# Attention with a spatial-gating MLP on one core: a stored order of the pieces, and weight bits in PSUM

## The chip, the cores and the metric

The kernel runs on one core of one Trainium2 chip. The metric is the device time of one execution in microseconds, and lower is better. A core has a TensorE (PE in the profile, with its weight loads as PEld), a VectorE (DVE), a ScalarE (ACT), a GpSimd (POOL) and a SyncE (SP), each with its own queue of instructions that it works off in order; SP here only issues DMAs. Engines wait for one another through semaphores.

## The reference

Eight batches, each with 8 heads of 64 over 576 positions. Attention is the sum of two parts, and an MLP with a gate over positions follows:

```python
q_d = q.reshape(B, H, Sd, 4, D).mean(axis=3)          # k_d and v_d alike; Sd = 144
out_up = np.repeat(sm_attn(q_d, k_d, v_d), 4, axis=2)  # softmax attention on the means of 4
scores = np.where(abs(i - j) < 4, scale * q @ k.T, -1e9)
out_local = softmax(scores) @ v                        # a band of 7 keys
x = out_up + out_local                                 # heads side by side: 576 x 512
h = gelu(x @ w_in)                                     # tanh form, 512 x 1024
u, v = h[..., :512], h[..., 512:]
v_n = (v - mean(v)) / sqrt(var(v) + 1e-6) * g_ln
v_s = einsum('ts,bsd->btd', w_sg, v_n) + b_sg[None, :, None]
out = x + (u * v_s) @ w_out
```

`w_in` and `w_out` arrive as 64-bit floats, so the kernel turns their two 32-bit words into one 32-bit float itself.

## The kernel before

**Pieces.** The work is cut into about 2200 pieces, each a few instructions on one engine. A piece has a name, the engines that can run it, the pieces it comes after, the buffers it takes and those it gives back. For a pair of heads `g` (32 of them, four for each batch), the pieces are: `lq lk lv lw` loads of q, k and two forms of v; `qs ks vs` sums of four; `S` scores of the band and `Y` scores of the means (PE); `ma mb` mask; `mx my` maxima; `nx ny` the scaled negative maxima used as bias; `ea eb ec` exponentials on ACT with their sums; `rc` reciprocal of the sums; `np nq` norms; `T U t` transposes on PE; `pa pb pc pe` their evacuation from PSUM; `d` and `D` products with v on PE; `od` mean part evacuated; `xa xb` the two parts added into x; `xh xl xc` x split into a high float and a low rest, since each large product is made of three (high times high, low times high, high times low). The first six pairs are "early": they take the mask and the sum of v into PE products.

For a batch `b`, five `v` products (the first half of the MLP's hidden layer), each followed by gelu `vg`, statistics `vb`, a root on POOL `vp`, `vn`, and a high and a low part `vh vl`; eight `u` products with gelu `ua`; eight gate products `s` with bias `sa` and gate `sm`, then parts `gh gl`; eight output products `o`, added to x (`oa`) and stored (`os`).

**Weights.** `w_in` and `w_out` come in 24 pieces of 128 x 256 (`y0` to `y7`, `z0` to `z7`, `r0` to `r7`). Each runs through `w` (load), `wb` (two DVE instructions, lines 345 and 347: shift and mask the high word into the bit pattern of a float), `wu` (ACT: the low word), `wq` (ACT: a square, for the test of small values), `wf` (DVE, line 361: flush small values to zero), `wt` (POOL or DVE, line 366: add both words), `wh` (high part) and `wl` (low part, line 372). All 24 run in the first batch, beside its attention. The bit pattern is held in a second buffer of the pool R, taken at the load together with the first. The five pieces `q0` to `q4` of the gate's matrix need only a high and a low part.

**Buffers.** Eight PSUM banks (`ps`), ten buffers `X` and forty buffers `R` are handed to the pieces as they come free.

**The order.** A planner, `plan`, runs when the kernel is built. It has a cost in us for each piece on each engine, due times worked back from the period of 70 us for a batch, limits on how many buffers each kind may hold (`CAPS`), and a string `ORDER` of 442 corrections in us to the pieces' latest start times, some with an engine named. It steps through time and gives each engine the ready piece with the earliest latest start. What comes out is a sequence of pieces with engines and buffers; each engine's queue holds its pieces in that sequence.

The lines that matter to the change are 330 to 381 (`weight64`), 541 to 544 (`recip`) and 645 to 686, where the pieces of a pair are declared. Line 788 is the helper of the products u, s and o, line 710 that of v, line 271 the helper of all copies.

Of the kernel before, what the change touches and what calls it, by code (L numbers as in the profile page):

```python
# [50 lines left out]
class Task:  # L51
# [4 lines left out]
    def __init__(self, name, engines, emit, after, takes=(), gives=(), due=None, func=None, mb=0.0, hold=0.0):  # L56
        self.name, self.engines, self.emit, self.due, self.func, self.mb = name, engines, emit, due, func, mb
        self.after, self.takes, self.gives, self.hold = list(after), list(takes), list(gives), hold
        self.kind = name.rstrip("0123456789.")
        if self.kind[0] == "w" and len(self.kind) > 2:  # L60
            self.kind = self.kind[:2]


LAT = 0.16
COLD = 0.8
AHEAD = 25.0
TABLE = 1.3
DMA_LAT, DMA_RATE = 1.9, 0.26

SHARED = dict(np=0.6, nq=0.6, xl=0.6, wb=1.0, wf=1.0, wt=1.0, wl=0.7, wh=1.0, vn=0.3, vh=1.0, vl=0.6,  # L70
              xh=1.0, sm=0.6, gh=1.0, gl=0.6, nx=0.3, ny=0.3)
LONE = ("vp", "xc")


def plan(tasks, sizes, caps, later={}, pinned={}):

    n = len(tasks)
    index = {t.name: i for i, t in enumerate(tasks)}
    succ, left = [[] for _ in tasks], [0] * n
    for i, t in enumerate(tasks):
        for a in set(t.after):
            succ[index[a]].append(i)
            left[i] += 1
    cost = [min(t.engines.values()) + (DMA_LAT + t.mb / DMA_RATE if t.mb else 0.0) for t in tasks]
    order, seen = [i for i in range(n) if not left[i]], list(left)
    for i in order:  # L90
        for j in succ[i]:
            seen[j] -= 1
            if not seen[j]:
                order.append(j)
    assert len(order) == n, [t.name for i, t in enumerate(tasks) if seen[i]][:20]
    due = [1e9 if t.due is None else t.due for t in tasks]
    for i in reversed(order):
        for j in succ[i]:
            due[i] = min(due[i], due[j] - cost[j] - LAT)
    latest = [due[i] - cost[i] + later.get(t.name, 0.0) for i, t in enumerate(tasks)]  # L100
    free = {p: list(range(c)) for p, c in sizes.items()}
    held = {k: 0 for k in caps}
    readers = {}
    for t in tasks:
        for g in t.gives:
            readers[g] = readers.get(g, 0) + 1
    engine_at = {e: 0.0 for t in tasks for e in t.engines}
    func_on, where, given, out = {}, {}, [], []
    dma_at = now = beside = 0.0
    idle = 1.0  # L110
    ready = [max(t.hold, latest[i] - AHEAD) if t.mb else t.hold for i, t in enumerate(tasks)]
    pending = [i for i in range(n) if not left[i]]

    def fits(t):
        need = {}
        for k in t.takes:
            need[k[0]] = need.get(k[0], 0) + 1
            need[k[:2]] = need.get(k[:2], 0) + 1
        return all(len(free[k]) >= c if k in free else k not in caps or held[k] + c <= caps[k]
                   for k, c in need.items())  # L120

    def engines(i):
        e = pinned.get(tasks[i].name)
        return {e: tasks[i].engines[e]} if e else tasks[i].engines


    def queue(e, i):
        total = 0.0
        for j in pending:
            if j != i and ready[j] <= now + 1e-9 and latest[j] < latest[i] and e == home[j]:  # L130
                total += tasks[j].engines[e]
        return total

    home = [min(engines(i), key=engines(i).get) for i in range(n)]
    while len(out) < n:
        while given and given[0][0] <= now + 1e-9:
            k = given.pop(0)[1]
            free[k[0]].append(where[k])
            if k[:2] in caps:
                held[k[:2]] -= 1  # L140
        best = None
        for i in pending:
            t = tasks[i]
            if ready[i] > now + 1e-9 or not fits(t):
                continue
            can = engines(i)
            ends = {e: max(now, engine_at[e]) + c + queue(e, i) for e, c in can.items()} if len(can) > 1 else can
            e = min(ends, key=ends.get)
            if engine_at[e] > now + 1e-9:
                continue  # L150
            key = latest[i] + (TABLE if t.func and func_on.get(e, t.func) != t.func else 0.0)
            if best is None or key < best[0]:
                best = key, i, e
        if best is None:
            times = [x for x in engine_at.values()] + [ready[i] for i in pending] + [g[0] for g in given]
            times = [x for x in times if x > now + 1e-9]
            assert times, ("stuck", sorted(tasks[i].name for i in pending)[:40], free)
            now = min(times)
            continue
        _, i, e = best  # L160
        t = tasks[i]
        pending.remove(i)
        end = now + t.engines[e]
        if e == "V" and t.kind in SHARED:
            end += SHARED[t.kind] * max(0.0, min(end, beside) - now)
        if e == "P" and t.kind not in LONE:
            beside = end
        if e == "T":
            idle = 0.85 * idle + 0.15 * min(1.0, (now - engine_at[e]) / 2.0)
            end += COLD * min(1.0, 3.0 * idle) * t.engines[e]  # L170
        if t.func:
            if func_on.get(e, t.func) != t.func:
                end += TABLE
            func_on[e] = t.func
# [26 lines left out]
wtz0,-42.5, wz1,4.5, wbz2,-37.5, wtz2,90,P wlz2,-57.5,P wz3,10.5, wtz3,17.5, wlz3,87.5,P wz4,8.5, wbz4,-121,
wfz4,14, wtz4,15.5, wz5,13, wuz5,-23.5, wqz5,-33, wtz5,-6,P wz6,-5.5, wfz6,-177, wz7,4, wfz7,-84.5, wr0,38,
wur0,77.5, wfr0,199.5, wtr0,37.5, wr1,-26, wbr1,43.5, wqr1,57.5, wbr2,24, wqr2,-36, wlr2,23,V wr3,-13.5, wbr3,1,
whr3,61.5, wr4,29, wqr4,52.5, wlr4,94.5,V wr5,-24, wbr5,25, wqr5,64, whr5,32.5,A wr6,42, wur6,-38.5, wqr6,-19,
wlr6,78,P wlr7,-18,P whq0,10.5, wlq0,-15,V wq1,10, whq1,-30.5,V wq2,-6, wq3,-11, lq0,-198.5,S lw0,-79,S
# [812 lines left out]
```

## Time and profile before

| | us |
|---|---|
| three runs | 627.39, 627.63, 629.62 |
| their median | 627.63 |
| the profiled execution | 627.54 |
| its span, first to last instruction | 625.8 |

| engine | busy us | share of the span | instructions |
|---|---|---|---|
| PE | 595.5 | 95% | 6600 |
| PEld | 532.9 | 85% | 6600 |
| DVE | 474.2 | 76% | 996 |
| ACT | 364.2 | 58% | 1262 |
| POOL | 275.0 | 44% | 359 |

The mean granted clock of TensorE is 0.988 of full speed. PE's matmuls are pipelined and overlap, and their ends are modelled, so a PE that is busy isn't PE at its peak. A share of busy time is a mean over stages: what a change is worth is read from the stage in which it acts. In a line of the groups stand the kernel's line, the engine, the operation, output and inputs by the program's names with their shapes, the count, then the busy time in us, the mean of one in ns, and the idle time of the engine just before them with what ended it.

### The profile page before, as it was taken

What the parts mean: (1) busy time and instruction counts of PE and PEld (TensorE: products, weight loads), DVE (VectorE), ACT (ScalarE), POOL (GpSimd) and SP (SyncE); (2) the same over time, 40 slices, a digit from 0 to 9 for tenths busy, and PEclk for the clock granted to TensorE, in tenths of its full rate; (3) what the DMA queues carried; (4) which work ended last, traced back from release to release, by engine and by line L of the source; (5) the groups of instructions that cost most, each with busy time, mean ns of one, the idle gap of its engine ahead of it and who ended that gap; (6) DMA issues with size and microseconds to landing.
All of it is one profiled execution on the core that took longest, in us unless ns stands there. A gap on an engine that the chain in (4) does not pass through costs nothing.

```text
span 625.8 us, 16764 instructions
## 1 busy us (share of the span) xinstructions
PE 595.5 (95%) x6600; PEld 532.9 (85%) x6600; DVE 474.2 (76%) x996; ACT 364.2 (58%) x1262; POOL 275.0 (44%) x359
## 2 busy tenths in 40 slices
PE   5788789799999999999999999999999999999998
PEld 3666589698899989998899989998899888989997
DVE  4999999965889587894969785784889678663553
ACT  3987778468682666555455646746684577811300
POOL 2485956613647144543535243652438355131410
PEclk9999899699999999999999999999999999999999
DMA  9963411426213304324212332034212222001002
GB/s 294 313 195 124 144 54 34 120 89 185 80 41 101 116 25 133 101 78 137 60 41 59 117 122 70 29 96 149 89 61 80 78 61 80 2 38 40 0 2 76
DMA packets 28495, 58.10 MB, mean 93 GB/s; under 512 B 3328, under 2 KB 3584, under 8 KB 28416
## 3 DMA queue, kind: packets, MB, share of 16 engines
q1 hardware_dynamic: 27648, 55.51, 28.5%
q10 hardware_dynamic: 768, 1.52, 0.7%
q8 instruction: 52, 0.85, 0.6%
q14 instruction: 27, 0.22, 0.1%
HBM read 47.58 MB, written 9.44 MB: 91 GB/s over the span
## 4 chain that ended last, share of the span: by engine, by line
PE 80%; DVE 13%; POOL 2%; issue 2%; ACT 1%; DMA 1%; POOLq 0%; DVEq 0%
PE ps L788 48%; PE ps L710 15%; PE ps L616 3%; PE ps L468 3%; PE ps L560 3%; PE ps L595 3%; PE ps L490 2%; PE ps L555 2%; DVE R L347 2%; DVE R L361 1%; DVE R L345 1%; POOL R L366 1%; DVE vs L825 1%; DVE R L550 1%; DMA R<-in_qT_dram 1%
## 5 line engine op out<-in xcount | busy, mean ns | idle before, releaser
L788 PE MATMUL ps<-wsg_h,R 128*128 128x288 f32 x576 | 123.0, 300 | 2.1 <-DVE wsg_h L271 2.0
L788 PE MATMUL ps<-R,wout_h 128*128 128x288 f32 x512 | 108.9, 300 | 0.0
L788 PEld LDWEIGHTS ps<-wsg_h,R 128*128 128x128 f32 x576 | 93.7, 188 | 4.7 <-DVE wsg_h L271 2.2
L788 PE MATMUL ps<-wsg_l,R 128*128 128x288 f32 x320 | 92.7, 296 | 0.5 <-DVE wsg_l L399 0.5
L530 ACT ACTIVATE X<-X,nb 128x64 f32<-128x64 f32 x260 | 86.8, 336 | 4.8 <-DVE nb L509 4.3
L788 PEld LDWEIGHTS ps<-R,wout_h 128*128 128x128 f32 x512 | 83.7, 188 | 2.7 <-issue 0.8
L788 PE MATMUL ps<-X,win_h 128*128 128x288 f32 x256 | 79.6, 311 | 1.8 <-ACT win_h L271 1.8
L788 PE MATMUL ps<-X,win_l 128*128 128x288 f32 x256 | 76.5, 299 | 1.5 <-POOL win_l L372 1.5
L788 PE MATMUL ps<-R,win_h 128*128 128x288 f32 x256 | 76.3, 298 | 0.0
L788 PE MATMUL ps<-R,wout_l 128*128 128x288 f32 x256 | 75.6, 295 | 0.0
L710 PE MATMUL ps<-win_h,X 128*128 128x512 f32 x160 | 65.3, 408 | 0.0
L710 PE MATMUL ps<-win_l,X 128*128 128x512 f32 x160 | 63.2, 395 | 0.0
L788 PEld LDWEIGHTS ps<-wsg_l,R 128*128 128x128 f32 x320 | 60.2, 188 | 0.7 <-DVE wsg_l L399 0.7
L751 POOL TENSOR_TENSOR rs<-rs,nhalf 128x1 f32<-128x1 f32 (+1 forms) x40 | 26.6, 666 | 67.5 <-DVE rs L742 67.4
L860 DVE TENSOR_TENSOR R<-ps,R 128x288 f32<-128x288 f32 x64 | 28.5, 452 | 34.9 <-PE ps L788 34.5
L271 ACT COPY R<-ps 72x288 f32<-72x288 f32 (+3 forms) x88 | 33.0, 418 | 34.7 <-PE ps L555 20.0
L788 PEld LDWEIGHTS ps<-X,win_h 128*128 128x128 f32 x256 | 48.9, 191 | 5.0 <-ACT win_h L271 2.1
L710 PE MATMUL ps<-win_h,R 128*128 128x512 f32 x128 | 50.6, 395 | 0.0
L788 PEld LDWEIGHTS ps<-X,win_l 128*128 128x128 f32 x256 | 48.8, 191 | 1.8 <-POOL win_l L372 1.8
L788 PEld LDWEIGHTS ps<-R,win_h 128*128 128x128 f32 x256 | 49.0, 191 | 0.2
L530 ACT ACTIVATION_READ_ACCUMULATOR X<-X,nb 128x1 f32 x260 | 48.9, 188 | 0.0
L788 PEld LDWEIGHTS ps<-R,wout_l 128*128 128x128 f32 x256 | 48.2, 188 | 0.1
(104 smaller groups left out, 1423.4 us busy)
## 6 DMA issues: line engine op xcount, KB each, us to landing
X<-in_vw_dram SPq DMA_DIRECT2D x31, 320.0 KB
R<-in_qT_dram SPq DMA_DIRECT2D x31, 293.0 KB
R<-in_kT_dram SPq DMA_DIRECT2D x31, 293.0 KB
out_dram<-R SPq DMA_DIRECT2D x31, 288.0 KB
R<-in_v_dram SPq DMA_DIRECT2D x60, 144.0 KB
R<-in_w_in_dram SPq DMA_DIRECT2D x16, 256.0 KB
R<-in_w_out_dram SPq DMA_DIRECT2D x8, 256.0 KB
R<-in_w_sgT_dram SPq DMA_DIRECT2D x5, 288.0 KB
```

What stands on the lines that cost most here:

```text
L271: (nc.scalar.copy if e == "A" else ENG[e].tensor_copy)(**kw)
L347: nc.vector.scalar_tensor_tensor(out=bits.bitcast(I32), in0=hw.bitcast(I32), scalar=-0x40000000, in1=bits.bitcast(I32), op0=ALU.bitwise_an ...
L468: nc.tensor.matmul(out=sp[i][os, c * KB:(c + 1) * KB], lhsT=q[hs, t * QB:t * QB + KB], rhs=k[hs, t * QB:t * QB + KB], start=not early, sto ...
L490: nc.tensor.matmul(out=st["sdv"][n][os], lhsT=qd2[par][hs, i * 48:i * 48 + HD], rhs=st["kd"][hs], start=True, stop=True)
L530: nc.scalar.activation(out=st["ms"][:, t, :], in_=src, func=AF.Exp, bias=st["nb"][:, i * NTP + c:i * NTP + c + 1], scale=scale, accum_out= ...
L560: nc.tensor.matmul(out=out[:, i * P:(i + 1) * P], lhsT=st["pd"][:, n, keys], rhs=ident2[:, i % 2], is_transpose=True, start=True, stop=True)
L595: nc.tensor.matmul(out=dn[hs].rearrange("p (i m) -> p i m", i=3), lhsT=st["v4"][kt][:, f, hs] if early else st["vd"][:, kt, hs], rhs=pdt[: ...
L616: nc.tensor.matmul(out=at["ps", "o", g, i][hs, c * QB:(c + 1) * QB], lhsT=v[ks, c, hs], rhs=pt[ks, c, h ^ i], start=True, stop=True)
L710: nc.tensor.matmul(out=acc, lhsT=r32(l), rhs=r32(w[:, k, DM:DF]), start=(i == 0 and ks[0] == 0), stop=(i == len(ops) - 1 and ks[-1] == KT ...
L751: nc.gpsimd.tensor_tensor(out=rs[0:n], in0=rs[0:n], in1=nhalf[0:n], op=ALU.pow)
L788: nc.tensor.matmul(out=acc[:, 0:HALF], lhsT=r32(l), rhs=r32(r), start=(first and n == 0), stop=(last and n == len(ops) - 1))
L860: nc.vector.tensor_tensor(out=x[:, half(i)], in0=at["ps", "m", b, "o", i][:, 0:HALF], in1=x[:, half(i)], op=ALU.add)
```

## The change

Three things are changed.

The planner, its costs, its due times and its caps go. `ORDER` is now the sequence itself, 2229 words, each a piece's name and, where there is a choice, its engine after a slash (S, V, A, P; T for PE needs none). `place` walks through it, hands out the buffers first come, first served, and returns the sequence. The order of pieces, the engines of some of them and the places of the loads in SP's queue differ from what the planner gave; the instructions of a piece don't, but for the two edits that follow.

The bit pattern of a weight piece is held in a PSUM bank from `wb` to `wf`: the shift and the mask write to PSUM and read there, and the flush reads PSUM and writes to a buffer R, which is taken only then.

The small constant that is added to the sums of the softmax leaves `rc` and becomes a piece of its own, `re`, on ACT (15 pairs) or DVE (17 pairs); `rc` keeps the reciprocal.

Over the whole sequence, against the planner's: `xl` on POOL for 23 pairs instead of 5, `vl` for 22 instead of 11, `gl` for 13 instead of 7, `ks` for 21 instead of 12, `np` for 13 instead of 10; on ACT `vh` 25 instead of 17, `gh` 18 instead of 14, `pc` 16 instead of 24, `wh` 14 instead of 19. The costs in the declarations are changed too, but nothing reads them any more.

```diff
+def place(tasks, sizes):
+    named = {t.name: t for t in tasks}
     free = {p: list(range(c)) for p, c in sizes.items()}
+    readers, where, order = {}, {}, []
     for t in tasks:
+        for k in t.gives:
+            readers[k] = readers.get(k, 0) + 1
+    for word in ORDER.split():
+        name, _, e = word.partition("/")
+        t = named.pop(name)
         for k in t.takes:
             where[k] = free[k[0]].pop(0)
+        for k in t.gives:
+            readers[k] -= 1
+            if not readers[k]:
+                free[k[0]].append(where[k])
+        order.append((t, e or next(iter(t.engines))))
+    assert not named
+    return order, where
...
 ORDER = """
+lk0/S ks0/V lq0/A qs0/V Y0 small wy7 wy2 wy0 lq1/A wby7 wqy7 wuy7 my0 wfy7 ny0/V wuy2 wuy0 ec0 qs1/P wty7/P lk1/S
+ks1/P wby0 wqy0 wy5 S0 mx0 wuy5 wby5 wfy0 wy3 lq2 wy1 lk2 lq3 wz5 b wr1 wz2 nx0/A ea0 S1 wy6 wy4 lk3 lk4 wz7 lq4
+lv0/S wz6 lw0/S wr2 wq3 lv1/S wz4 wby3 qs2/P wty0/P Y1 mx1 wq2 lk5 lw1/S wz1 wz0 wuy3 my1 eb0 wqy3 wqy5 nx1/V re0/V
+rc0 ny1/V why7/V wfy3 why0/V wfy5 ks2/P np0/P ea1 nq0/P S2 ec1 wby2 eb1 wqy2 mx2 wuy4 lq5 wuy1 T0 pa0/V wty5/P
+why5/V U0 pb0/V nx2/V re1/V qs3/P wfy2 Y2 pc0/A rc1 wby4 my2 ks3/V ea2 ny2/V t0 pe0/A nq1/P np1/P eb2 ec2 wty2/P
+wty3/P ks4/P S3 qs4/V wby6 mx3 wqy4 wqy6 wfy4 wfy6 t1 T1 wuz5 U1 wuy6 pa1/A re2/A pb1/A d0 wby1 rc2 nx3/A Y3 why2/V
+np2/V pc1/A wqy1 wty4/P why4/V wfy1 wbz4 my3 wly7/V ea3 od0 wty6/P lw2 wuz7 pe1/A T2 pa2/A nq2/P D0 wly0/P xa0
+wly5/P wqz4 U2 t2 wfz4 wur2 ny3/A why6/A wuz4 ec3 wuz6 wty1/P pb2/V wly4/P d1 wbz5 pc2/V xb0 why1/V wqz5 eb3 xh0/V
...
+v0.2 D4 vg0.1 vb0.1 whq0/A wqr5 wfr5 v0.3 vg0.2 xa4 vb0.2 xb4 ks7/P Y7 S6 v0.4 whq1/A vg0.0 whq4/A
...
+u0.3 ua0.3 vl0.2/V Y6 T5 wbr2 wur4 wqr2 wfr7 my6 whr1/A xc4 pa5/V s0.0 sa0.0 ks8/P wtr7/P sm0.0/P wlr5/P wlr1/P ec7
...
+sm0.7/P wlr2/P sm0.6/P wtr4/P wlr0/V whr4/V d5 Y8 U6 gh0.2/A my8 lw6 od5 lv6 gh0.3/A gl0.2/P D5 lw7 gl0.3/V T6 xa5
+S7 ma7 mb7 mx7 pa6/A pb6/A wlr6/P wlr4/P o0.6 ny8/A ec8 vs6 lq9 o0.3 t6 o0.0 xb5 pc6/V pe6/V xh5/V xl5/P xc5 nx7/A
...
-        keys = ("R", "w", t, 0), ("R", "w", t, 1)
+        keys = ("R", "w", t, 0), ("R", "w", t, 1), ("ps", "b", t)
...
         def shift(e):
-            lw, hw, bits = words()
+            lw, hw, _ = words()
+            bits = buf(*keys[2])[:, 0:n]
             nc.vector.tensor_scalar(out=bits.bitcast(I32), in0=hw.bitcast(I32), scalar1=3,
                                     scalar2=0x3FFFFFF8, op0=ALU.logical_shift_left, op1=ALU.bitwise_and)
...
         def flush(e):
+            buf(*keys[1])
             lw, hw, bits = words()
             nc.vector.scalar_tensor_tensor(out=bits, in0=hw, scalar=F64_MIN * F64_MIN,
-                                           in1=bits, op0=ALU.is_ge, op1=ALU.mult)
+                                           in1=at[keys[2]][:, 0:n], op0=ALU.is_ge, op1=ALU.mult)
...
+        def total(e):
+            if e == "A":
+                nc.scalar.activation(out=sums[par], in_=sums[par], func=AF.Copy, bias=SM_EPS)
+            else:
+                nc.vector.tensor_scalar(out=sums[par], in0=sums[par], scalar1=SM_EPS, scalar2=None, op0=ALU.add)
+
         def recip(e):
             rc = st["rc"] = rc2[par]
-            nc.vector.tensor_scalar(out=rc, in0=sums[par], scalar1=SM_EPS, scalar2=None, op0=ALU.add)
-            nc.vector.reciprocal(out=rc, in_=rc)
+            nc.vector.reciprocal(out=rc, in_=sums[par])
...
-    order, spots = plan(tasks, SIZES, CAPS, later, pinned)
+    order, spots = place(tasks, SIZES)
     where.update(spots)
     with tc.manual_schedule():
-        for t, e, *_ in order:
+        for t, e in order:
             t.emit(e)
```

More of the change, by code (lines that the diff above doesn't have):

```diff
@@ L1 @@
-from bisect import insort
 from contextlib import ExitStack
@@ L51 @@
 class Task:
[L56 to L100, printed above, removed]
+    def __init__(self, name, engines, emit, after, takes=(), gives=(), func=None, mb=0.0):
+        self.name, self.engines, self.emit, self.func, self.mb = name, engines, emit, func, mb
+        self.after, self.takes, self.gives = list(after), list(takes), list(gives)
@@ L101, in plan @@
+def place(tasks, sizes):
+    named = {t.name: t for t in tasks}
     free = {p: list(range(c)) for p, c in sizes.items()}
-    held = {k: 0 for k in caps}
-    readers = {}
+    readers, where, order = {}, {}, []
     for t in tasks:
[L105 to L174, printed above, removed]
@@ L201 @@
[L201 to L205, printed above, removed]
@@ L372, in low @@
             ENG[e].tensor_tensor(out=r32(lo), in0=words()[2], in1=hi, op=ALU.subtract)
-        add(f"w{t}", {"S": 0.5}, load, takes=keys, mb=0.26, hold=W_HOLD[t[0]])
-        add(f"wb{t}", {"V": 0.66}, shift, [f"w{t}"])
+        add(f"w{t}", {"S": 0.5}, load, takes=keys[:1], mb=0.26)
+        add(f"wb{t}", {"V": 0.88}, shift, [f"w{t}"], takes=keys[2:])
         add(f"wu{t}", {"A": 0.36}, units, [f"w{t}"])
         add(f"wq{t}", {"A": 0.34}, square, [f"wb{t}"])
-        add(f"wf{t}", {"V": 0.33}, flush, [f"wq{t}"])
-        add(f"wt{t}", {"P": 0.75, "V": 0.6}, total, [f"wf{t}", f"wu{t}"])
+        add(f"wf{t}", {"V": 0.43}, flush, [f"wq{t}"], takes=keys[1:2], gives=keys[2:])
+        add(f"wt{t}", {"P": 0.75, "V": 0.7}, total, [f"wf{t}", f"wu{t}"])
         add(f"wh{t}", {"A": 0.36, "V": 0.26}, high, [f"wt{t}"])
-        add(f"wl{t}", {"P": 0.9, "V": 0.36}, low, [f"wh{t}"], gives=keys, due=W_DUE[t[0]])
+        add(f"wl{t}", {"P": 0.9, "V": 0.36}, low, [f"wh{t}"], gives=keys[:2])
     for t, w, h, l, off in (("y", w_in, win_h, win_l, DM), ("z", w_in, win_h, win_l, 0),
@@ L693, in mlp @@
         first = b == 0
-        base = BASE + b * PERIOD
         xn = [f"xl{b * NPAIR + p}" for p in range(NPAIR)]
@@ L879, in mlp @@
                         takes=[] if k else [("ps", "m", b, "v", s)])
-                add(N("v", s), {"T": c / KT}, v_mm(s, range(k + 1, KT)), xn[-1:] + w[-2:] + [f"vk{s}.{k}"], due=end_at, gives=xs)
+                add(N("v", s), {"T": c / KT}, v_mm(s, range(k + 1, KT)), xn[-1:] + w[-2:] + [f"vk{s}.{k}"], gives=xs)
             else:
-                add(N("v", s), {"T": c}, v_mm(s), xn + w + (xc if last else []), takes=[("ps", "m", b, "v", s)], due=end_at,
+                add(N("v", s), {"T": c}, v_mm(s), xn + w + (xc if last else []), takes=[("ps", "m", b, "v", s)],
                     gives=xs)
@@ L901, in mlp @@
             add(N("ua", i), {"A": 0.38}, u_act(i), [N("u", i), N("ua", i - 1) if i % 2 else None], takes=[("R", "us", b, i // 2)] if i % 2 == 0 else [],
-                gives=[("ps", "m", b, "u", i)], func="g", due=end_at + 4)
+                gives=[("ps", "m", b, "u", i)], func="g")
         for i in range(2 * KT):
-            end_at += 1.87 * f
             w = [f"wlq{s}" for s in range(NS)] + ["b", "small"] if first else []
-            add(N("s", i), {"T": 1.93}, s_mm(i), [N("vl", s) for s in range(NS)] + w,
-                takes=[("ps", "m", b, "s", i)], due=end_at,
+            add(N("s", i), {"T": 1.95}, s_mm(i), [N("vl", s) for s in range(NS)] + w,
+                takes=[("ps", "m", b, "s", i)],
@@ L924, in mlp @@
                 w = [f"ok{i}"]
-            add(N("o", i), {"T": 1.64 * len(ks) / KT}, o_mm(i, ks), [N("gl", d) for d in range(KT)] + w, takes=take, due=end_at,
+            add(N("o", i), {"T": 1.66 * len(ks) / KT}, o_mm(i, ks), [N("gl", d) for d in range(KT)] + w, takes=take,
                 gives=[("R", c, b, d) for c in ("gh", "gl") for d in range(KT)])
```

229 lines of the change are left out of this document (128 added, 101 removed).

## The prediction

> **What bounds the kernel now.** I read the page's slices first, then the busy times by stretch, then TensorE's waits, then the groups of VectorE. The slices say where time is lost:
>
> ```profile
> PE   5788789799999999999999999999999999999998
> DVE  4999999965889587894969785784889678663553
> ```
>
> A slice is 15.6 us. TensorE (PE) has holes in the first eight or nine slices only; there VectorE (DVE) stands at 9 from the second slice to the eighth. The stretches put numbers to it (columns: length, then busy time and instructions of PE, PE's weight loads, DVE, ACT, POOL; then PE's granted clock, DMA share, GB/s):
>
> ```profile
> 0.00:20.00 20.00, 11.04 (x179) 7.37 (x179) 10.08 (x27) 10.55 (x57) 5.11 (x14) 1.00 0.92 312
> 20.00:40.00 20.00, 17.34 (x312) 13.04 (x312) 19.69 (x45) 17.86 (x86) 13.10 (x17) 1.00 1.00 286
> 40.00:60.00 20.00, 17.76 (x246) 13.30 (x247) 19.48 (x47) 16.30 (x71) 13.35 (x18) 1.00 0.35 109
> 60.00:80.00 20.00, 15.62 (x155) 13.03 (x154) 18.53 (x37) 13.44 (x33) 18.47 (x23) 0.91 0.40 129
> 80.00:100.00 20.00, 17.55 (x130) 16.85 (x128) 19.72 (x40) 16.54 (x46) 11.98 (x13) 1.00 0.23 69
> 100.00:120.00 20.00, 15.57 (x161) 13.46 (x161) 19.55 (x38) 10.94 (x32) 12.30 (x15) 0.82 0.33 93
> 120.00:140.00 20.00, 20.00 (x282) 18.06 (x283) 14.79 (x30) 11.74 (x56) 5.79 (x10) 0.93 0.19 61
> 300.00:400.00 100.00, 99.89 (x1122) 90.14 (x1121) 76.91 (x168) 59.29 (x217) 39.90 (x56) 1.00 0.25 76
> ...
> 0.00:126.90 126.90, 101.77 (x1258) 83.05 (x1258) 113.21 (x240) 89.42 (x336) 78.74 (x102) 0.95 0.51 158
> 126.90:626.00 499.10, 493.75 (x5345) 449.82 (x5343) 361.01 (x757) 274.74 (x927) 196.22 (x258) 1.00 0.24 76
> ```
>
> From 20 to 120 us DVE is busy 96.97 of 100 us and PE 83.84: DVE sets the pace and PE loses 16.2 us to it, at a clock granted down to 0.91 and 0.82. After that PE is busy 99.89 of 100 us, DVE 76.91. I cut at 126.9 because the chain of waits is unbroken PE work from about there:
>
> ```profile
> 126.96 3.40 PE ps L788 x24
> ```
>
> These are two output products of batch 0, pieces o0.0 and o0.7. From o0.0 on PE needs 493.75 us of work and loses 5.35. The kernel is thus a start-up that DVE bounds and 499 us that PE bounds. PE's order is nearly kept and its instructions are the same, so the second part can hardly get shorter; the question is when o0.0 starts. Who PE waited for in the start-up agrees: producers on or behind DVE late by some 2 us each, and a first wait of 6.4 us for data, which nothing here moves much:
>
> ```profile
> PE ps L490 <- DVE kd L435: 6.4, 1, 6.4
> PE ps L595 <- ACT R L271: 2.7, 3, 2.2
> PE ps L788 <- DVE wsg_h L271: 2.0, 1, 2.0
> ```
>
> **The bit patterns in PSUM.** All 24 weight pieces are unpacked on DVE in the start-up (lines 345, 347, 361). The groups up to 126.9 us, with those that the reordering moves (count | busy us, mean ns):
>
> ```profile
> L347 DVE SCALAR_TENSOR_TENSOR R<-R,R 128x256 int32<-128x256 int32 x24 | 15.4, 641 | 0.8
> L361 DVE SCALAR_TENSOR_TENSOR R<-R,R 128x256 f32<-128x256 f32 x24 | 12.9, 559 | 0.0
> L345 DVE TENSOR_SCALAR R<-R 128x256 int32<-128x256 int32 x24 | 9.7, 404 | 0.0
> L271 DVE COPY R<-ps 72x288 f32<-72x288 f32 (+2 forms) x12 | 5.9, 493 | 0.2 <-PE ps L555 0.2
> L623 DVE TENSOR_TENSOR R<-ps,od 128x290 f32<-128x290 f32 x12 | 5.3, 446 | 0.3 <-PE ps L616 0.3
> L844 DVE TENSOR_TENSOR R<-R,R 128x576 fp32r<-128x576 f32 x4 | 4.3, 1082 | 0.0
> L779 DVE TENSOR_TENSOR R<-R,R 128x512 fp32r<-128x512 f32 x4 | 3.9, 974 | 0.0
> L825 DVE SCALAR_TENSOR_TENSOR vs<-ps,small_sb,b_sb 128x288 f32<-128x288 f32 x8 | 3.9, 496 | 0.0
> L547 DVE TENSOR_TENSOR X<-X,rc 128x640 f32<-128x640 f32 x4 | 3.3, 818 | 0.0
> L635 DVE TENSOR_TENSOR R<-R,X 128x576 fp32r<-128x576 f32 x3 | 2.8, 925 | 0.0
> L543 DVE TENSOR_SCALAR rc<-sums 128x13 f32<-128x13 f32 x7 | 2.2, 315 | 2.4 <-ACT X L530 1.4 <-ACT R L538 1.0
> L271 DVE CAST wout_h<-R 128x256 fp32r<-128x256 f32 x4 | 2.2, 558 | 0.0
> L509 DVE TENSOR_SCALAR nb<-stats 128x10 f32<-128x10 f32 x5 | 1.9, 382 | 0.1
> L544 DVE RECIPROCAL rc<-rc 128x13 f32<-128x13 f32 x7 | 1.7, 241 | 0.2
> ```
>
> The three weight groups take 15.4 + 12.9 + 9.7 = 38.0 us. One and the same instruction takes 0.42 or 1.53 us, and the long one starts inside a POOL instruction and ends just after it:
>
> ```profile
> 21.79 0.28 DVE L345 TENSOR_SCALAR R<-R 128x256 int32<-128x256 int32 x1
> 22.10 0.42 DVE L347 SCALAR_TENSOR_TENSOR R<-R,R 128x256 int32<-128x256 int32 x1
> ...
> 41.83 1.47 POOL L635 TENSOR_TENSOR R<-R,X 128x576 fp32r<-128x576 f32 x1
> 42.05 1.53 DVE L347 SCALAR_TENSOR_TENSOR R<-R,R 128x256 int32<-128x256 int32 x1
> ```
>
> So DVE waits for POOL on these lines. It doesn't on lines that have one operand in PSUM: L623 (290 elements) means 446 ns and L825 (288) 496 ns, while POOL was busy 78.74 of 126.9 us. After the change each of the three has an operand in PSUM. Nearest rows: 256 elements at L347's undisturbed 0.42 us give 3 x 0.42 x 24 = 30.2 us (the first, 0.28 in SBUF, would cost 0.42, since nothing here shows a PSUM form at the fast rate); at L825's 0.496, less its 32 extra elements (0.04), 0.46 x 72 = 33.1 us. The gain is 4.9 to 7.8 us; I take 6. If POOL still holds them up, only the slower first line is left: 24 x 0.14 = 3.4 us lost. These are the bounds.
>
> A rule of the Trainium skill speaks against this edit: VectorE: DVE Perf Modes ("Why PSUM operands drop a tier", and the cycle table of its errata section) gives up the double rate for fp32 with an operand in PSUM and adds some 62 cycles, about 65 ns at its clock. By that the weights would cost an estimated 34.9 us, the gain on them be 3.1 and the time 618. Another one, GPSIMD Engine Reference ("Specifications"), lets the two engines collide only where DVE works at the two-port rate or reads two inputs from SBUF; by that rule all three lines are free afterwards, and the trace agrees (446 against 1530 ns).
>
> The cost: a bank of the eight PSUM banks from shift to flush. In the new list one or two weights hold one at a time, three once, and no bank is taken within four places of a flush that frees it; I cost it at nothing, hidden by those places, and if a PE piece does wait, the wait is one flush, 0.46 us. A second buffer R per weight is now taken only at the flush, which lets loads start earlier.
>
> **The stored order.** The list names the engine of each piece, so what stands ahead of o0.0 on DVE can be counted, old against new. Gone to POOL or ACT, or later: two x-low pieces (L635, 2 x 0.93), one s-gate low part (L844, 1.08), one v-low (0.97), one norm (L547, 0.82), three biases (L509, 3 x 0.38), seven evacuation copies less four added short ones (L271 on PSUM, net 1.8), and eight single pieces of 0.3 to 0.75 each against two added, net 3.0. Added: five weight casts (L271, 5 x 0.51 = 2.5, from 0.558 and shorter). The epsilon is now added by a piece of its own, `re`: DVE had 7 x (0.315 + 0.241) = 3.9 us and keeps 7 x 0.241 + 3 x 0.315 = 2.6; four go to ACT, which was busy only 89.42 of 126.9. The moves sum to 9.4 us less. POOL gets five pieces more ahead of o0.0 (seven low parts, norms and sums against two), about 6 us: 85 against 78.74.
>
> DVE's bill ahead of o0.0 is 113.2 - 6 - 9.4 = 97.8 us, 15.4 less. Its idle time there, 126.9 - 113.2 = 13.7 us (9.9 of it in the first 20), need not fall. PE's own limit: of its holes after 20 us, 16.2, all could go, and some 3 us of slow clock. So 15.4 is near what PE can give. I take 12 of it, because the new list also moves loads: it puts 24 transfers ahead of the first v load `lv0`, which used to be issued at once.
>
> ```profile
> GB/s 294 313 195 124 144 54 34 120 89 185 80 41 101 116 25 133 101 78 137 60 41 59 117 122 70 29 96 149 89 61 80 78 61 80 2 38 40 0 2 76
> ...
> R<-in_qT_dram SPq DMA_DIRECT2D x31, 293.0 KB
> ...
> R<-in_w_in_dram SPq DMA_DIRECT2D x16, 256.0 KB
> ...
> 1.66 1.17 ACTq L426 DMA_DIRECT2D R<-in_v_dram  x2
> ```
>
> Twelve weights at 0.256, ten q and k at 0.293 and two of similar size are 6.7 MB, 22 us at the 0.3 MB/us of the first slices, so PE's first d piece cannot start before about 24 us. That costs PE up to 3 us between 20 and 40, while DVE works on weights; hence 15.4 - 3.
>
> After o0.0 DVE carries less than before (about 40 us go to POOL over the whole run, chiefly 18 x-low, 11 v-low and 6 gate-low pieces), so it won't become the bound; PE is saturated and has 5.35 us to lose or win, its closing wait for the last store included. I change nothing there.
>
> **Sum.** Span 625.8 - 12 = 613.8; the profiled execution took 627.54, 1.74 more than its span, and the median of the runs is 627.63, the same within 0.1. Forecast 627.54 - 12 = 615.5 us.
>
> **Rivals.**
>
> (a) All of PE's holes after 20 us close: 16.2 plus about 3 of slow clock, 608 us. For it: DVE's saving of 15.4 and its own early idle 9.9 that more weight work can fill. Against: the later v loads.
>
> (b) DVE's time isn't what the edit says: the PSUM forms are held up by POOL all the same, or pay the slower rate. Then +3.4 in place of -6, and POOL's 6 us more disturb the other SBUF pieces: 15.4 - 9.4 - 2 - 3 (loads) leaves 1 us; about 626.5, no change. L623 and L825 speak against it, but no row shows DVE writing to PSUM.
>
> (c) Slower. POOL becomes the late engine in the PE-bound part. Its forms are slow:
>
> ```profile
> L635 POOL TENSOR_TENSOR R<-R,X 128x576 fp32r<-128x576 f32 x5 | 7.6, 1511 | 15.5 <-ACT X L271 9.3 <-DVE X L271 6.2
> L844 POOL TENSOR_TENSOR R<-R,R 128x576 fp32r<-128x576 f32 x7 | 10.8, 1542 | 18.4 <-ACT R L271 9.3 <-DVE R L271 9.1
> ```
>
> The 35 moved low parts each end about 0.6 us later than on DVE (1.51 against 0.93), and behind each stand, on the same queue, the v sums and norms of the next pair. PE takes its pieces in a fixed order, so one late input stops all. At 0.6 us this is 21 us if all of it reaches PE; from 12 us on, that is more than half, the start-up's gain is gone, and at all of it the time is 615.5 + 21 = 636. Against it: POOL is busy 39.90 of 100 us in the steady stretches, and the moved parts, 35 x 1.53 over five such stretches, add 11 to that.
>
> **Chances.** My forecast's case (gain 6 to 16, 611 to 621): 0.62. (a): 0.14. (b) and smaller gains between: 0.16. (c): 0.08. The range for 8 in 10 runs from (a)'s side, 607, to just short of (b), 625. About 0.5% (3 us) is what a measurement of this kernel can tell from no change; below 624.5 lie the first case, (a) and the part of (b) where some of the gain is left, 0.06: 0.82; within 3 us the rest of (b), 0.10; slower (c), 0.08.
>
> **What would show it.** Right: L345, L347 and L361 mean 0.40 to 0.46 us with little spread, L361 and L347 no longer stretched to a POOL instruction's end; DVE's busy time ahead of o0.0 near 98 us; o0.0 starting near 115; PE busy 99% from there, clock 1.00 after 100 us. Wrong: means of 0.55 us and more on these lines (b); PE waiting for POOL lines 635, 779, 844 or 453 between 130 and 600 us (c); PE idle by 5 us and more for L595 around 24 to 45 us (the loads).

## The result, and the profile after

The changed kernel took a median of 613.81 us (four runs, 612.97 to 614.55) against 627.51 for the kernel before, run beside it: a ratio of 0.977, 95% interval 0.975 to 0.979. Run again beside three of the kernels below it was 616.01 (six runs, 613.82 to 618.76) against 628.05, 0.981 (0.978 to 0.984). These executions spread over 4.9 us, those of the kernel before over 2.9. The longer ones have the lower mean clock of TensorE (0.997 to 1.000 in the three up to 615.01 us, 0.986 to 0.992 in the three from 617.01 on); the last section comes back to it. The profiled execution took 612.97 us with a span of 611.2.

The stretches of the kernel after, with the columns of those shown before (length, then busy time and instructions of PE, PEld, DVE, ACT, POOL; PE's granted clock, DMA share, GB/s):

```profile
20.00:40.00 20.00, 16.82 (x308) 12.77 (x308) 19.40 (x54) 19.36 (x98) 15.02 (x21) 0.98 1.02 294
40.00:60.00 20.00, 20.00 (x278) 15.99 (x275) 18.91 (x48) 17.34 (x79) 17.93 (x23) 1.00 0.72 204
60.00:80.00 20.00, 20.00 (x205) 18.02 (x204) 18.81 (x43) 14.01 (x30) 13.78 (x16) 1.00 0.14 43
80.00:100.00 20.00, 18.67 (x145) 17.54 (x144) 18.85 (x39) 15.10 (x57) 13.09 (x16) 1.00 0.16 48
100.00:120.00 20.00, 19.48 (x309) 17.50 (x308) 14.99 (x28) 10.29 (x47) 14.21 (x18) 1.00 0.43 139
300.00:400.00 100.00, 100.00 (x1174) 91.62 (x1173) 74.67 (x144) 56.36 (x225) 60.51 (x75) 1.00 0.26 82
...
0.00:110.00 110.00, 96.46 (x1249) 80.06 (x1250) 95.80 (x226) 82.12 (x336) 77.16 (x103) 0.98 0.61 187
110.00:611.50 501.50, 494.80 (x5354) 450.31 (x5351) 341.78 (x704) 253.09 (x926) 246.40 (x311) 1.00 0.24 75
```

From 20 to 120 us PE is busy 94.97 of 100 us; it was 83.84. Piece o0.0 starts at 110.0 instead of 126.9 us, 16.9 earlier. From there to the end it takes 501.2 us (the last 0.3 of the row lies behind the span) where it took 498.9: 2.3 us are given back. 16.9 - 2.3 = 14.6 is the difference of the spans. A second profiled execution of the same kernel has o0.0 at 111.2 us and 501.2 behind it, so a difference of one us at o0.0 between two kernels is no more than one kernel shows by itself.

The groups of the three weight lines (shift 296, mask 298, flush 313), up to 110 us:

```profile
L298 DVE SCALAR_TENSOR_TENSOR ps<-R,ps 128x256 int32<-128x256 int32 x24 | 10.3, 429 | 0.8
L296 DVE TENSOR_SCALAR ps<-R 128x256 int32<-128x256 int32 x24 | 10.0, 416 | 2.5 <-DMA R<-in_w_in_dram 2.5
L313 DVE SCALAR_TENSOR_TENSOR R<-R,ps 128x256 f32<-128x256 f32 x24 | 9.8, 411 | 0.8 <-ACT R L308 0.7
```

30.1 us in all, 38.0 before; the long ones are gone. And PE's waits after (total, times, longest):

```profile
PE ps L442 <- DVE qd L387: 6.1, 1, 6.1
PE ps L512 <- DVE R L313: 2.3, 2, 1.9
...
PE ps L743 <- DVE X L428: 1.6, 1, 1.6
...
PE ps L512 <- POOL X L504: 0.5, 1, 0.5
```

The second is new: a transpose (T2) waits for a PSUM bank that a flush gives back. The third and the fourth lie behind o0.0.

### The profile page after: what moved, and what is told of

Same layout as the page of the kernel before. It is cut to its first block, busy times and chain, and to the rows that moved or that the text cites. A ratio compares the mean times of both kernels' runs of the same rounds, so it can differ in the third digit from the quotient of the medians.

```text
span 611.2 us, 16757 instructions
## 1 busy us (share of the span) xinstructions
PE 591.3 (97%) x6600; PEld 530.4 (87%) x6600; DVE 437.6 (72%) x930; ACT 335.2 (55%) x1260; POOL 323.6 (53%) x414
## 4 chain that ended last, share of the span: by engine, by line
PE 83%; DVE 9%; DMA 4%; ACT 2%; POOL 1%; issue 1%; ACTq 0%; POOLq 0%
PE ps L743 48%; PE ps L665 17%; PE ps L552 4%; PE ps L573 3%; PE ps L517 3%; PE ps L420 3%; PE ps L512 2%; PE ps L442 2%; DMA R<-in_w_in_dram 2%; DMA R<-in_qT_dram 2%; DVE R L714 2%; DVE R L787 1%; ACT X L482 1%; PE ps L522 1%; DVE R L734 1%
## 5 line engine op out<-in xcount | busy, mean ns | idle before, releaser
L706 POOL TENSOR_TENSOR rs<-rs,nhalf 128x1 f32<-128x1 f32 (+1 forms) x40 | 24.6, 616 | 83.8 <-DVE rs L697 83.8
L592 POOL TENSOR_TENSOR R<-R,X 128x576 fp32r<-128x576 f32 x23 | 34.0, 1479 | 35.8 <-ACT X L222 21.0
L222 ACT CAST R<-R 128x512 fp32r<-128x512 f32 (+2 forms) x43 | 27.4, 640 | 44.1 <-DVE R L714 20.1
L404 POOL TENSOR_TENSOR pairs<-R 72x256 f32<-72x256 f32 x52 | 45.5, 875 | 11.3 <-DMA R<-in_v_dram 11.1
L780 DVE SCALAR_TENSOR_TENSOR vs<-ps,small_sb,b_sb 128x288 f32<-128x288 f32 x64 | 32.4, 510 | 22.7 <-PE ps L743 21.5
```

The source lines that it names most:

```text
L222: (nc.scalar.copy if e == "A" else ENG[e].tensor_copy)(**kw)
L404: ENG[e].tensor_tensor(out=pairs, in0=v[:, 0:2], in1=v[:, 2:4], op=ALU.add)
L592: ENG[e].tensor_tensor(out=r32(st["xl"]), in0=st["x"][:, 0:S], in1=st["xh"][:, 0:S], op=ALU.subtract)
L706: nc.gpsimd.tensor_tensor(out=rs[0:n], in0=rs[0:n], in1=nhalf[0:n], op=ALU.pow)
L780: nc.vector.scalar_tensor_tensor(out=vsb[i], in0=at["ps", "m", b, "s", i][:, 0:HALF], scalar=g_sb[:, i // 2:i // 2 + 1], in1=b_sb[:, half( ...
```

## The experiments

Line numbers shift by a few from kernel to kernel; the forms name the work.

**The old sequence as a list.** The sequence of the planner is written into the list, with its engines; the bits stay in the buffers R. It separates the way of storing from what is stored.

```diff
-        keys = ("R", "w", t, 0), ("R", "w", t, 1), ("ps", "b", t)
+        keys = ("R", "w", t, 0), ("R", "w", t, 1)
...
-            bits = buf(*keys[2])[:, 0:n]
+            bits = buf(*keys[1])[:, 0:n]
```

> The planner's old sequence stored as a list, bits in SBUF, the added epsilon as its own piece on DVE just ahead of rc: only the buffers that the pieces get can differ. Every theory: 626 to 629, o0.0 near 127. If not, the handing out of buffers is part of the effect.

628.55 us (ten runs) against 627.85: 1.001 (0.9998 to 1.0022). The stretch to its o0.0:

```profile
0.00:127.80 127.80, 103.99 (x1257) 85.86 (x1257) 113.79 (x240) 88.84 (x334) 78.11 (x101) 0.92 0.51 156
```

127.8 us and 113.79 of DVE, as before the change (126.9, 113.21). The storing, the handing out of buffers and `re` as a piece of its own are worth nothing that these runs can tell (0.7 us). This is the base of the next one.

**The old sequence, 15 of the 24 weights in PSUM.** The old sequence has no free bank for the other nine.

```diff
-            bits = buf(*keys[2])[:, 0:n]
+            bits = buf(*keys[2 if held else 1])[:, 0:n]
```

> The planner's old sequence, stored as a list, with the bits of 15 of the 24 weights in PSUM; for the other 9 no bank is free between shift and flush in that sequence, and their bits stay in SBUF. Theory: 15 x 0.33 = 5 us less on DVE ahead of o0.0, which comes 3 to 5 us earlier than 126.9; 622 to 625. Rival (in the old sequence PE waits for the order, not for DVE's speed): 626 to 628.5.

626.18 us (ten runs), 0.9964 (0.995 to 0.9977): 2.4 us below the one above, and in the rival's range, not in the theory's. Groups and stretch:

```profile
L297 DVE SCALAR_TENSOR_TENSOR ps<-R,ps 128x256 int32<-128x256 int32 x15 | 6.4, 429 | 0.5
L297 DVE SCALAR_TENSOR_TENSOR R<-R,R 128x256 int32<-128x256 int32 x9 | 6.1, 678 | 0.3
L313 DVE SCALAR_TENSOR_TENSOR R<-R,ps 128x256 f32<-128x256 f32 x15 | 6.0, 411 | 0.0
L313 DVE SCALAR_TENSOR_TENSOR R<-R,R 128x256 f32<-128x256 f32 x9 | 5.1, 580 | 0.0
...
0.00:124.10 124.10, 102.35 (x1258) 85.09 (x1258) 107.28 (x238) 88.04 (x330) 75.96 (x100) 0.93 0.51 161
```

In one kernel and one start-up the same line takes 429 ns with an operand in PSUM and 678 without, the flush 411 and 580. The form with PSUM keeps its time inside a POOL instruction too:

```profile
85.01 1.28 POOL L734 TENSOR_TENSOR R<-R,R 64x512 fp32r<-64x512 f32 x1 [1.60 <-ACT R L220]
...
85.58 0.43 DVE L297 SCALAR_TENSOR_TENSOR ps<-R,ps 128x256 int32<-128x256 int32 x1
```

DVE's bill falls by 6.5 us against the list above and o0.0 comes 3.7 earlier (2.8 against 126.9, where 3 to 5 were expected). In the old order a part of what DVE saves reaches the time, not all.

**The new list, bits in an SBUF buffer.** All 24 bit patterns go to a spare buffer X instead of a bank; the list is that of the change. (SBUF has no room for buffers of their own: the pool would take 120.5 kb per partition, and 119.2 are left.)

```diff
-        keys = ("R", "w", t, 0), ("R", "w", t, 1), ("ps", "b", t)
+        keys = ("R", "w", t, 0), ("R", "w", t, 1), ("X", "b", t)
```

> The new list, unchanged, but the bit pattern lies in a spare SBUF buffer X from shift to flush instead of a PSUM bank. Theory (DVE's bill sets the start-up, POOL holds up DVE's SBUF forms): the three weight lines go from 429, 416 and 411 ns back to 0.55 to 0.65, 0.35 to 0.42 and 0.50 to 0.58 us, 4 to 8 us more on DVE ahead of o0.0. Issuing one weight instruction twice, 8 us more on DVE, has since cost 3.7 us of time, so by the same theory 2 to 4 us here: 615.5 to 618. Rival (the list does it all, the place of the bits is worth nothing): 613 to 615.

625.97 us (ten runs) against 628.53 before: 0.9948 (0.9928 to 0.9967). That is 8 us above the upper end of the theory's range, and further above the rival's. Its weight groups and the stretch to o0.0:

```profile
L298 DVE SCALAR_TENSOR_TENSOR X<-R,X 128x256 int32<-128x256 int32 x24 | 20.2, 841 | 0.8
L313 DVE SCALAR_TENSOR_TENSOR R<-R,X 128x256 f32<-128x256 f32 x24 | 14.5, 609 | 0.6 <-ACT R L308 0.5
L296 DVE TENSOR_SCALAR X<-R 128x256 int32<-128x256 int32 x24 | 11.7, 488 | 2.0 <-DMA R<-in_w_in_dram 2.0
...
0.00:123.90 123.90, 103.03 (x1249) 84.37 (x1250) 110.45 (x226) 85.05 (x345) 82.40 (x103) 0.93 0.53 169
```

So the new list alone is worth 2.6 us. In it the SBUF forms cost 46.4 us, 8.4 more than in the old sequence, and 16.3 more than the PSUM forms: the list puts POOL's work beside the weights. DVE's bill to o0.0 differs by 110.45 - 95.80 = 14.65 us from the change's, o0.0 by 13.9. The two parts of the change are each worth some 2 to 4 us alone (2.4 for 15 weights is 3.8 for 24 by proportion) and 12 to 14 together: the list moves work to POOL, which pays little as long as the weights collide with POOL.

The expectation counted 4 to 8 us more on DVE, half of it in the time. What it missed besides the size is that the hold-up goes both ways. The costliest group of POOL up to o0.0, first in this kernel, then in the changed one:

```profile
L318 POOL TENSOR_TENSOR R<-R,R 128x256 int32<-128x256 int32 x23 | 19.9, 874 | 6.7 <-DVE R L313 3.7 <-DVE nbd L473 2.7 <-DMA R<-in_kT_dram 0.4
```

```profile
L318 POOL TENSOR_TENSOR R<-R,R 128x256 int32<-128x256 int32 x23 | 18.0, 792 | 4.7 <-DVE nbd L473 3.0 <-DVE R L313 1.7
```

POOL's bill is 82.40 against 77.16 us for the same pieces, and PE waits 4.2 us for norms on POOL (line 504) ahead of o0.0, where the profile of the changed kernel shows no wait for POOL. PE's clock is lower here too, 0.93 against 0.98, and its busy time 6.6 us longer (103.03 against 96.46). That isn't the whole of it: the two executions with the highest mean clock, 0.994, still took 623.02 and 623.36 us.

**The old sequence behind o0.0.** New list as far as o0.0, then the planner's sequence and engines.

```diff
-o0.0 xb5 pc6/V pe6/V xh5/V xl5/P xc5
+o0.0 lk9 xb5 xh5/A pc6/A pe6/A nx7/V
```

> The new list up to o0.0, and everything not yet done in the planner's old sequence with its old engines. After o0.0 the changed kernel takes 501.2 us to the end, the old one 498.9. Theory (the second part is PE-bound in either order, and its 2.3 us are the new list's own waits): o0.0 at 110, the rest 498 to 500, time 610 to 612.5. Rival (start-up's gain is partly borrowed, work put off past o0.0 that must be caught up): the rest 501 to 505 in this order too, time 613 to 618.

613.31 us (four runs), 0.9767 (0.9743 to 0.9791), the same as the whole change. The two stretches:

```profile
0.00:110.80 110.80, 95.63 (x1250) 79.57 (x1250) 96.81 (x229) 81.63 (x327) 78.06 (x104) 1.00 0.58 180
110.80:611.30 500.50, 494.70 (x5353) 450.00 (x5351) 359.83 (x757) 276.52 (x936) 198.35 (x262) 1.00 0.24 76
```

All of the gain is made ahead of o0.0. In this kernel it takes 500.2 us from there to the end (611.0 - 110.8), 1.0 less than in the changed kernel and 1.3 more than before: between the theory's 498 to 500 and the rival's 501 to 505. Whether the 1.3 us are work put off past o0.0 isn't shown. Behind o0.0 the new list takes 18 us off DVE and 23 off ACT and puts 48 on POOL, and PE gains nothing by that.

**The v loads early.** `lv0` and `lw0` are issued right behind `lk1`, ahead of most weights.

```diff
-lk1/S ks1/P wby0
+lk1/S lv0/S lw0/S ks1/P wby0
```

> The new list with the loads lv0 and lw0 moved up to right behind lk1. In the changed kernel PE starts d0 at 27.0, 5.2 us later than in the old one, and is idle 3.2 us between 20 and 40. Prediction's step (the late v loads cost up to 3 us): d0 2 to 5 us earlier, o0.0 1 to 3 us earlier, time 611 to 613. Rival (PE catches up anyway, or the weights that land later starve DVE): 613 to 617.

616.84 us (four runs, 614.64 to 620.42), 0.983 (0.979 to 0.987). The row of d0 in the timeline, first of the changed kernel, then of this one:

```profile
27.04 2.18 PE L552 MATMUL ps<-R,R 72*64 72x144 f32 x32
```

```profile
4.73 0.75 SPq L375 DMA_DIRECT2D R<-in_v_dram  x2
...
27.64 2.18 PE L549 MATMUL ps<-R,R 72*64 72x144 f32 x32
```

The v loads are issued at 4.7 us instead of 17.2, and d0 starts at 27.6 instead of 27.0, in both without a wait of its own. It isn't late data that puts d0 behind the 21.8 of before. It stands behind other pieces of PE's queue: in both orders d0 follows T1 and U1, but the list puts S3 and t1 ahead of these, and T1 waits 0.98 us for exponentials on ACT. The weights pay for the moved loads (DVE waits 1.30 us for one at 13.2 us). The time is in the rival's range; o0.0 came at 115.2, behind a start-up with a clock of 0.93, so it can't be compared.

**Nineteen low parts on DVE.** The 19 `xl` that the list gives to POOL behind o0.0 go to DVE. It tests the slower rival, POOL as the late engine.

```diff
-xl5/P
+xl5/V
...
-xl31/P
+xl31/V
```

> The new list, but the 19 x-low pieces that it gives to POOL after o0.0 run on DVE at the same places. Prediction's side (POOL's later ends don't reach PE): 612.5 to 615. Rival (c) (the second part's 2.3 us are POOL's late pieces): 610 to 612. If DVE is the tighter engine there, 615 to 620.

611.97 us (four runs, 610.9 to 617.08), 0.9763 (0.9721 to 0.9805). The profiled execution is the longest of the four, 617.08; its wait ahead of T2, its second part and the clock of its start-up:

```profile
32.15 1.12 PE L509 MATMUL ps<-small_sb,X 128*128 128x128 f32 x4 [1.92 <-DVE R L310]
...
116.40:615.50 499.10, 494.56 (x5353) 450.23 (x5351) 347.62 (x723) 253.00 (x925) 221.54 (x292) 1.00 0.24 75
30.00:35.00 5.00, 3.08 (x51) 2.35 (x48) 4.34 (x9) 3.94 (x19) 3.73 (x5) 0.68 1.03 376
35.00:40.00 5.00, 5.00 (x38) 4.30 (x36) 4.40 (x14) 3.54 (x19) 2.31 (x3) 0.50 0.99 307
40.00:45.00 5.00, 5.00 (x76) 3.55 (x76) 0.93 (x3) 1.88 (x7) 1.86 (x3) 0.50 0.84 244
```

From o0.0 to the end it takes 498.9 us: the 2.3 us are back. Its start-up has the same pieces in the same order as the change's and takes 6.4 us more, at half the clock for ten us; this comes back below.

**Four low parts on DVE.** Of the nineteen only `xl8` to `xl11`, which stand in the stretch where the two gaps lie. Beside it, on the same chip, the changed kernel again (the 616.01 us of the result).

```diff
-xl8/P ... xl9/P ... xl10/P ... xl11/P
+xl8/V ... xl9/V ... xl10/V ... xl11/V
```

> Only the four low halves xl8 to xl11 go from POOL to DVE; the fifteen other ones stay on POOL. If the 2.3 us that the rest of the time lost came from these four (the gaps of PE before T10 and before o1.6 lie between d11 and s2.0), the time from o0.0 to the end is 499 us as with all nineteen on DVE, and the time is 611.0 to 612.0 us. If it is the sum over all nineteen, it is 612.5 to 613.5 us, with the gap before o1.6 still there.

> The changed kernel itself, as the base of the three beside it. 613 to 614 us; if the half-speed clock that was seen behind the 1.9 us hole of PE (31.8 us) in other kernels of this list is a matter of chance in each execution, one or two of the timed ones may lie at 617 to 618 with a mean clock of about 0.989, the others at 613 with 0.997.

612.01 us (four runs, 610.43 to 612.39), 0.9733 (0.9712 to 0.9755) against 0.9808 for the change beside it. From o0.0 to the end it is 499.0 us, so the four are the whole of the 2.3. (The medians differ by 4.0 us; behind o0.0 the edit accounts for 2.2 of them, and the four executions here all have a mean clock of 0.996 or more.) What they did is in the timelines around 186 us. The changed kernel:

```profile
186.00 1.43 POOL L592 TENSOR_TENSOR R<-R,X 128x576 fp32r<-128x576 f32 x1
...
186.33 1.12 DVE L473 TENSOR_SCALAR nbd<-stats 128x3 f32<-128x3 f32 x1
187.37 0.48 DVE L428 TENSOR_TENSOR X<-ps,small_sb 128x320 f32<-128x320 f32 x1
...
187.99 0.38 PE L743 MATMUL ps<-R,wout_h 128*128 128x288 f32 x1 [1.59 <-DVE X L428]
```

The kernel with four on DVE:

```profile
186.50 0.17 DVE L470 TENSOR_SCALAR nbd<-stats 128x3 f32<-128x3 f32 x1
186.58 0.48 DVE L425 TENSOR_TENSOR X<-ps,small_sb 128x320 f32<-128x320 f32 x1
...
187.21 0.37 PE L740 MATMUL ps<-R,wout_h 128*128 128x288 f32 x1 [0.16 <-DVE X L425]
...
111.40:610.70 499.30, 494.54 (x5354) 450.29 (x5351) 341.56 (x708) 253.18 (x926) 241.92 (x307) 1.00 0.24 75
```

`xl10` on POOL runs from 186.00 to 187.43. DVE's instruction on three numbers, 0.17 us otherwise, starts inside it, lasts 1.12 and ends at 187.45. Behind it stands the masking piece `mb12`, which frees the bank that o1.6 needs: PE waits 1.59 us. POOL was not late; it held DVE up, as it did the weights before the change. The instruction accounts for 0.95 of the 1.43 us by which the wait shrinks; by the rest DVE is further ahead of PE already when it starts, for which no cause is shown. The second profile of the changed kernel has the same 1.12 us inside `xl10`. The other gap, 0.49 us ahead of T10, is a true wait for a norm on POOL (line 504), and it is gone too.

**The first weight instruction twice.** A dose of DVE time, nothing else.

```diff
+            for _ in range(2):
-            nc.vector.tensor_scalar(out=bits.bitcast(I32), in0=hw.bitcast(I32), scalar1=3,
+                nc.vector.tensor_scalar(out=bits.bitcast(I32), in0=hw.bitcast(I32), scalar1=3,
```

> The changed kernel with the first weight instruction on DVE issued twice, the second writing the same bits: 24 x about 0.34 = 8 us more on DVE ahead of o0.0. Theory (DVE still sets the start-up): o0.0 5 to 8 us later, time 618 to 622. Rival (the start-up is now near PE's own limit, DVE has slack): o0.0 less than 3 us later, time under 617.

617.48 us (four runs, 617.06 to 621.34), 0.9853 (0.9817 to 0.9889).

```profile
L297 DVE TENSOR_SCALAR ps<-R 128x256 int32<-128x256 int32 x48 | 20.2, 422 | 3.1 <-DMA R<-in_w_in_dram 2.3
...
0.00:114.20 114.20, 99.33 (x1250) 81.72 (x1250) 103.27 (x250) 83.41 (x337) 77.32 (x103) 0.97 0.58 180
```

The line takes 10.2 us more, DVE's bill to o0.0 7.5, and o0.0 starts 4.2 us later than in the first profile of the change, 3.0 later than in the second: between the two forecasts, and so is the time. About half of added DVE time (0.4 to 0.56) is thus still on the path, a rough figure, since the clock alone moves o0.0 by some us; the other half fits into its idle time (110 - 95.80 = 14.2 us, and 114.2 - 103.27 = 10.9 here).

**The hole of T2 filled.** The flush of y1 goes ahead of `why4` on DVE, `od0` ahead of `ea3` on ACT, D0 ahead of T2 on PE, and T2 takes the flush's bank.

```diff
-np2/V pc1/A wqy1 wty4/P why4/V wfy1 wbz4 my3 wly7/V ea3 od0 ... pe1/A T2 pa2/A nq2/P D0
+np2/V pc1/A wqy1 od0 wty4/P wfy1 D0 T2 ea3 why4/V wbz4 my3 wly7/V ... pe1/A pa2/A nq2/P
```

> In the start-up five pieces change places: the flush of weight y1 goes ahead of why4 on DVE, the copy od0 ahead of the exponentials ea3 on ACT, and D0 ahead of T2 on PE, which takes another bank. D0 then runs in the hole that T2 left (29.86 to 31.77 us). If the wait for the bank is a cost, the hole falls from 1.9 to about 0.4 us and o0.0 starts 0.5 to 1.5 us earlier: 612.0 to 613.0 us. If something behind it (the DVE chain to d1) is what sets the pace, o0.0 stays at 110.0 and the time at 613.8. If the half-speed clock follows from the hole, no execution shows it: all within 1 us and a mean clock of 0.995 or more; if it has another cause, one or two of some seven lie 4 to 5 us higher.

614.26 us (six runs, 612.85 to 616.86), 0.978 (0.9757 to 0.9803), against 0.9808 for the change beside it; the intervals overlap.

```profile
29.26 0.81 PE L570 MATMUL ps<-R,X 64*64 64x58 f32 x40
30.46 0.66 PE L509 MATMUL ps<-small_sb,X 128*128 128x128 f32 x4 [0.39 <-DVE R L310]
...
33.48 2.18 PE L549 MATMUL ps<-R,R 72*64 72x144 f32 x32 [1.16 <-DVE R L577]
...
0.00:109.70 109.70, 96.41 (x1248) 79.64 (x1249) 95.99 (x226) 82.35 (x336) 77.18 (x103) 0.98 0.59 187
```

The wait for the bank falls from 1.9 to 0.39 us, and a wait of 1.16 for the DVE piece that gives d1 its bank (line 577, `xa0`) takes its place. o0.0 starts 0.3 us earlier, less than two executions of the changed kernel differ by (110.0 and 111.2), so no gain is shown. The bank that a weight holds has hardly a price here: a wait for DVE's queue comes in the place of the other. And the executions still differ by 4 us, at mean clocks of 0.992 to 1.000, so without the hole they don't become alike.

**Both edits.** Four low parts on DVE, and the hole filled.

> Both edits: xl8 to xl11 on DVE and the hole filled. If the two act in different stretches and add, 610.0 to 611.0 us, below both kernels of the case. If the DVE time of the four low halves is given back elsewhere, 612 us or more.

611.19 us (six runs, 610.81 to 614.32), 0.974 (0.9716 to 0.9765): below the kernel before and below the change on the same chip (0.9808, 0.978 to 0.9836). The four low parts alone do as well within the intervals, so what is shown is their gain. The profiled execution is one of the two longer ones, 614.25:

```profile
41.65 1.92 PE L549 MATMUL ps<-R,R 72*64 72x144 f32 x19 [1.40 <-issue]
...
113.20:612.70 499.50, 494.75 (x5354) 450.41 (x5351) 341.45 (x708) 253.04 (x926) 241.29 (x307) 1.00 0.24 75
40.00:45.00 5.00, 3.60 (x26) 2.56 (x23) 4.49 (x11) 4.39 (x26) 3.75 (x4) 0.75 1.00 286
```

Here PE stops for 1.40 us in the middle of one product, d2, waiting for nothing that the profile shows, and the clock dips behind that.

## Why the prediction was right, and where it wasn't

615.5 us was forecast, 613.81 and 616.01 were measured.

*What bounds.* Right in the main: a start-up that DVE sets and a rest that PE fills. The graft shows that the gain lies ahead of o0.0 alone. That DVE sets the start-up was read from its busy time and from three waits of PE. All the waits listed for PE up to 127 us, without the first, sum to 18.6 us: DVE ended 8.5 of them, ACT 5.2 and POOL 4.9. By the dose, about half of a us on DVE reaches o0.0 after the change.

*The weights.* The mechanism was right. The gain was 7.9 us, just beyond the good end of the 4.9 to 7.8 given, so the 6 was low: the end by L347's undisturbed 0.42 us was the right row, not L825's 0.496. The Trainium skill's page "VectorE: DVE Perf Modes" (Why PSUM operands drop a tier, and the cycle table of the errata section) is half borne out: the shift takes 416 ns in PSUM against the 0.28 us shown in SBUF, but the 65 ns more for each instruction aren't there (the flush takes 411 ns from PSUM and 0.41 us undisturbed in SBUF), and the 618 us by it were too high. The Trainium skill's rule of when the two engines collide ("GPSIMD Engine Reference", Specifications) agrees with the 429 against 678 ns of one line. L473's 1.12 us, with one input in SBUF, fit it only if that instruction ran at the two-port rate, which no run shows.

What the step did not see is that this edit and the list need one another. Costed against the old sequence, the weights save 8 us of DVE; in the new list, which sets more POOL work beside them, they would have cost 46.4 us, and the PSUM saves 16.3. The sum came out because the moves were costed without the collisions that they would have caused.

*The bank.* Costed at nothing. PE does wait for a flush, 1.9 us once and 0.4 once, longer than the one flush of 0.46 that was allowed for. T2 stands ten places behind that flush in the list, but places in the list don't say when DVE's queue gets there: ahead of the flush it had a norm of 1.52 us and a cast of 0.81, which take 0.82 before the change and 0.28 at their shortest here; both lie beside POOL instructions. Filling the hole gives no gain that can be told, so nothing was about right for the time.

*The moves.* 9.4 us off DVE were forecast. DVE's bill without the weight lines went from 113.21 - 38.0 = 75.2 to 95.80 - 30.1 = 65.7: 9.5. That the two agree to 0.1 is luck: the four full scalings of v (line 759, then 714) fell from 6.1 to 3.6 us without being in the sum, and three norms (line 547, then 504) now take 1.28 us each, not 0.82. The bill of 97.8 became 95.80, and DVE's idle time stayed (13.7 and 14.2), as the step let it. POOL was put at 85 us ahead of o0.0; it was 77.16, below the 78.74 of before. POOL gets shorter instructions where DVE leaves it alone: the sums of weight words (line 366, then 318) took 924 ns each before, 792 after, and 874 in the new list with the bits in X.

*The late loads.* This step failed. It took 3 us off for v loads that come late. d0 did start at 27.0, as "not before about 24 us" has it, yet moving the loads ahead by 12 us brings it no earlier, and PE doesn't wait for it. Without this step the forecast of o0.0 is 126.9 - 15.4 = 111.5; it started at 110.0.

*After o0.0.* "I change nothing there" was off by 2.3 us. The third rival had the engine, POOL, and its mechanism in the smaller gap, 0.49 us for a late norm. In the larger one, 1.59 us, no low part was late; one held a small DVE instruction up until it ended, just where a bank was due. POOL's share of a steady stretch was put at 39.90 + 11 us of 100; it is 60.51.

The gain of 16.9 and the loss of 2.3, where 12 and 0 stood, make 14.6 against 12: two errors that partly cancel, so a part of the forecast's closeness is luck. The clock's share, which the first rival put at about 3 us and the forecast left out, is in the 16.9: PE's busy time ahead of o0.0 fell by 5.3 us, from 101.77 to 96.46, for nearly the same pieces, and the granted clock rose from 0.95 to 0.98.

What stays open is why PE's clock dips in some executions of one program and not in others, and what the 1.40 us with no releaser in the last kernel were. The 16 DMA engines were busy throughout that stretch (a share of 1.00 in its row); whether PE's instructions came late behind the data was not tried.

## What to carry to other kernels

Where VectorE and GpSimd share a stage, look for instructions that start inside a GpSimd instruction and end with it, whatever their size; here an operand in PSUM freed the VectorE instruction of it, and the GpSimd work beside it got shorter too. Moving work to GpSimd was worth 2.6 us as long as the two collided and was part of 12 to 14 once they didn't. So cost such a pair of edits together, with each alone as a check. And when work goes to an engine "with time to spare", ask not only whether it is late, but whom it holds up while it runs.
